# Transposing DMAs no longer serialized with plain DMAs, and two parameter loads in place of a touch read, in a statically scheduled SSM + SwiGLU kernel

## The chip, the cores and the metric

The kernel runs on one core of one Trainium2 chip. The metric is the device time of one execution in microseconds (us). The kernel before scattered by at most 0.33% within one set of rounds (179.78 to 180.37 us in the widest). A profile shows one execution, so where a kernel scatters it need not show the median one. Engines in the profile: PE is TensorE's matmuls, PEld its weight loads, DVE is VectorE, ACT is ScalarE, POOL is GpSimd, SP is SyncE, which here only issues DMAs. "SPq" and "ACTq" are DMA issues on the queue of that engine.

## The reference, cut to what matters

```python
# x: 2048 x 512; P = 512 complex states; F = 1376; everything bfloat16
x  = A_x
xn = _layernorm(x)
# A: diagonal state space model
Lam_bar = exp(exp(log_dt) * (Lambda_re + 1j*Lambda_im))
Bu   = xn @ (((Lam_bar - 1) / Lam)[:, None] * (B_re + 1j*B_im)).T
h    = scan over rows t:  h = Lam_bar * h + Bu[t]
a    = 2 * real(hseq @ (C_re + 1j*C_im).T) + xn * Dskip
# B: gated feed-forward
b    = (silu(xn @ w_gate) * (xn @ w_up)) @ w_down
out  = x + a + b
```

## The kernel before

The 2048 rows are 16 tiles of 128 rows, worked on in four chunks of four tiles. Each chunk needs: its load; the layer norm's statistics on VectorE and the norm itself (on ScalarE for chunks 2 and 3); a transpose of the normalized rows by DMA; the gate, up and B projections on TensorE; evacuations of PSUM by ScalarE (it copies TensorE's results out of tile `pb`, so that the next matmuls may write there); the rotation and scan on VectorE; and one accumulation on TensorE of the down projection ("dA") and of the state times the C weights ("dB"). The C weights (tile `W`) are computed once, on ScalarE and VectorE, from the transposed C (tile `hss`, lent for it) and the parameters.

Nothing is ordered by hand. The program is a graph of tasks; a list scheduler with a model of durations puts the tasks of ACT, DVE and POOL in an order, and PE and SP keep the order in which the program names them. Only then are the waits put in. So the instruction order on ScalarE and VectorE is an output of a model of when DMAs land. The parts that matter:

```python
_DMA_BW = 330.0        # bytes per ns in the model
_DMA_LAT = 2000.0      # ns
_CHAIN = ("pe", "sp")  # these keep program order
...
        # in _schedule, for the best candidate t of engine e that could start at st:
        if t.dma:
            issue_done = st + t.est
            xs = max(st + min(t.est, 300.0), dma_free[e])
            dma_free[e] = xs + t.nbytes / (_DMA_BW if e == "sp" else 0.5 * _DMA_BW)
            t.fin = dma_free[e] + _DMA_LAT
            free[e] = issue_done
...
        dma_tasks = []
        xp_state = [None]

        def dma(name, dst, src, writes, nbytes, ..., xpose=False, ...):
            after = tuple(after)
            if xpose:
                after = after + tuple(dma_tasks)          # a transpose waits for every DMA before it
                fn = ... dma_start_transpose ...
                est, nb = 2000.0, int(nbytes * 1.2)
            else:
                if xp_state[0] is not None:
                    after = after + (xp_state[0],)        # a plain DMA waits for the last transpose
                fn = ... dma_start ...
                est, nb = 330.0 + nbytes / 900.0, nbytes
...
        x_load(0)
        x_load(1)
        act_q = [dma("ld_touch", tch[0:16], wg_v[0:128:8, :, 0:2], [("tch",)], 16 * 16, eng="act")]
        act_q.append(wg_load("a0", 0, 2, eng="act", order=(act_q[-1],)))     # 448 KB of gate weights
        x_load(2)
        act_q.append(wg_load("a1", 2, 3, eng="act", order=(act_q[-1],)))     # 224 KB
        wg_load("a2", 3, 4)
        x_load(3)
        pload("ld_ldt", 2, A_log_dt)           # 1 KB each
        pload("ld_lim", 1, A_Lambda_im)
        pload("ld_lre", 0, A_Lambda_re)
        # then: up weights, rest of the gate weights, x tiles 4-7 ("x4"), B_re and B_im (transposes),
        # chunk 1's rows (transpose), C_re and C_im (transposes), x tiles 8-11 ("x8"), down weights, ...
...
        streams = _schedule(g.tasks, engs)      # fixes the order on ACT, DVE, POOL
        _plan(g.tasks, streams, new_sem, eng_sems)   # puts the semaphore waits in
```

The touch is a small read of `w_gate` (16 partitions, 8 elements each); nothing uses its result.

Of the kernel before, what the change touches and what calls it, by code (L numbers as in the profile page):

```python
# [12 lines left out]
B16 = mybir.dt.bfloat16  # L13
# [236 lines left out]
def bass_parallel_sum__ssm_conv_s5__swiglu_ffn__prompt_kernel(  # L250
# [23 lines left out]
    KT = D // 128  # L274
# [6 lines left out]
    g = _Graph()  # L281
    es = ExitStack()
    with es:
        block = es.enter_context(nc.Block(no_gpsimd_drain=True))

        def sb(name, shape, dt):
            return es.enter_context(nc.sbuf_tensor(name, shape, dt))
# [41 lines left out]
        st0 = sb("st0", [128, 4, 2, 6], F32)  # L329
        sd0 = sb("sd0", [128, 4], F32)  # L330
        epst = sb("epst", [128, 1], F32)
        tch = sb("tch", [16, KT, 2], B16)
        praw = sb("praw", [128, 3, PT], B16)
        prow = sb("prow", [12, 128], B16)
        ecst = sb("ecst", [128, PT], F32)
# [1 line left out]
        NSM = 64  # L337
        sm = sb("sm", [128, NSM, PT], F32)
# [46 lines left out]
        wg_v = B_w_gate.rearrange("(k p) f -> p k f", p=128)  # L385
        wu_v = B_w_up.rearrange("(k p) f -> p k f", p=128)

        dma_tasks = []
        xp_state = [None]

        def dma(name, dst, src, writes, nbytes, reads=(), after=(), out_=False, eng="sp", xpose=False, prio=0.0, order=(), **kw):
            after = tuple(after)
            if xpose:
                after = after + tuple(dma_tasks)
                fn = lambda e, dst=dst, src=src: e.dma_start_transpose(out=dst, in_=src)
                est, nb = 2000.0, int(nbytes * 1.2)
            else:
                if xp_state[0] is not None:
                    after = after + (xp_state[0],)
                fn = lambda e, dst=dst, src=src: e.dma_start(dst, src, **kw)  # L400
                est, nb = 330.0 + nbytes / 900.0, nbytes
            t = g.add(eng, fn, reads=reads, writes=writes, name=name, dma=True, after=after, out=out_, est=est, nbytes=nb, prio=prio, order=order)
            dma_tasks.append(t)
            if xpose:
                xp_state[0] = t
            return t

        TILEB = 128 * D * 2
# [4 lines left out]
        def pload(name, slot, src, **kw):  # L413
            return dma(name, prow[4 * slot:4 * slot + 4, :], src.rearrange("(a p) -> a p", p=128), [("prow", slot)], 1024, **kw)

        def x_load(a, **kw):
            return dma("ld_x%d" % a, x_sb[:, a:a + 1, :], x_v[:, a:a + 1, :], [("x", a)], TILEB, **kw)

        def wg_load(nm, k0, k1, **kw):
            return dma("ld_wg" + nm, wg[:, k0:k1, 0:FG], wg_v[:, k0:k1, 0:FG], [("wg", nm)], (k1 - k0) * 128 * FG * 2, **kw)  # L420

        x_load(0)
        x_load(1)
        act_q = [dma("ld_touch", tch[0:16], wg_v[0:128:8, :, 0:2], [("tch",)], 16 * 16, eng="act")]
        act_q.append(wg_load("a0", 0, 2, eng="act", order=(act_q[-1],)))
        x_load(2)
        act_q.append(wg_load("a1", 2, 3, eng="act", order=(act_q[-1],)))
        wg_load("a2", 3, 4)
        x_load(3)
        pload("ld_ldt", 2, A_log_dt)  # L430
        pload("ld_lim", 1, A_Lambda_im)
        pload("ld_lre", 0, A_Lambda_re)
        dma("ld_wu0", wu[:, :, 0:FH0], wu_v[:, :, 0:FH0], [("wu", 0)], 512 * FH0 * 2)
        dma("ld_wg1", wg[:, :, FG:Fh], wg_v[:, :, FG:Fh], [("wg", 1)], 512 * (Fh - FG) * 2)
# [7 lines left out]
        def loads_stage_b2():  # L442
# [13 lines left out]
              reads=[("ones",)], writes=[("ident",)], name="ident", est=300)  # L456
        g.add("pool", lambda e: e.iota(iot[:], pattern=[[1, TP]], base=0, channel_multiplier=0, allow_small_or_imprecise_dtypes=True),
              writes=[("iot",)], name="iota", est=1000)
# [1 line left out]
        g.add("pool", lambda e: e.memset(car[:, 0], 0.0), writes=[("car", 0, 0), ("car", 0, 1)], name="car0", est=100)  # L460
        g.add("pool", lambda e: e.memset(ecst[:], math.e), writes=[("ecst",)], name="ecst", est=100)
        def act_table(func, order):
            g.add("act", lambda e: e.activation(out=sm[:, NSM - 1, 0:1], in_=epst[:], func=func, bias=epst[:, 0:1]), reads=[("epst",)], writes=[("sm", "_warm")],
                  name="act_warm", est=1500, order=order)

        act_table(AF.Sqrt, (act_q[-1],))

        def pe_warm(n, w=512, bk=None):
# [295 lines left out]
        def ffn_gate_quarters(pairs):  # L764
# [27 lines left out]
            for a_, b_ in zip(seq, seq[1:]):  # L792
                hold[b_].od.add(hold[a_])
            act_table(AF.Silu, (hold["ev21"],))
            hold["evac"] = g.tasks[-1]
            ffn_mm(0, NQ, "g", xt_pair[0])
# [275 lines left out]
```

## Time and profile before

| | before |
|---|---|
| time, median of 3 | 179.94 us (179.92 to 180.0) |
| profiled span | 178.1 us |
| PE busy | 174.4 us (98%) |
| DVE busy | 162.3 us (91%) |
| waits of PE | 0.8 us, at the start only |
| x4 landed / x8 landed | 13.76 us / 40.26 us |
| last C weight ready / first dB matmul | 73.08 us / 75.06 us |

The busy shares, from the first part of the page:

```profile
PE 174.4 (98%) x929; PEld 84.1 (47%) x937; DVE 162.3 (91%) x281; ACT 88.8 (50%) x114; POOL 10.3 (6%) x21
```

All of PE's waits, from the view of waits. The columns are: what waited, on what, us in total, times, longest us.

```profile
PE pb L474 <- PEq L1057: 0.8, 1, 0.8
```

Two places of the chain that ended last, the first PE piece and the very end. The columns are start, length in us, and what it was. Between them the chain is PE throughout:

```profile
7.01 0.28 PE pb L568 x2
...
170.59 5.18 PE pb L953 x39
175.79 0.29 DVE x_sb L958
```

So TensorE is the bound: at the pace of this chain (64 projection matmuls in 13.81 us, 216 ns each, at a granted clock of 1.0) there is nothing to gain from 7.01 us to 175.8 us without taking matmuls away.

SP's timeline shows what serializing costs in DMA time. The columns are start, length of the issue, queue and line, operation and tiles:

```profile
5.81 0.55 SPq L400 DMA_DIRECT2D x_sb<-in_A_x_dram  x1
14.00 2.06 SPq L395 DMA_TRANSPOSE BT<-in_A_B_re_dram  x1
18.54 2.00 SPq L395 DMA_TRANSPOSE BT<-in_A_B_im_dram  x1
22.90 1.78 SPq L395 DMA_TRANSPOSE xnT<-xn_sb  x1
28.54 1.70 SPq L395 DMA_TRANSPOSE hss<-in_A_C_re_dram  x1
32.63 1.97 SPq L395 DMA_TRANSPOSE hss<-in_A_C_im_dram  x1
36.79 0.37 SPq L400 DMA_DIRECT2D x_sb<-in_A_x_dram  x1
```

Each transpose is issued only when all earlier loads have landed, so x8 is issued at 36.79 us. The statistics of those tiles stand late on VectorE, so it waits only 0.76 us for them (in brackets: idle before, and what ended it):

```profile
40.28 2.47 DVE L479 BATCH_NORM_STATS2 st<-x_sb 128x6 f32<-128x512 bf16 x4 [0.76 <-DMA x_sb<-in_A_x_dram]
```

The PSUM evacuations (L839, L841, L844) and the first silu of chunk 1 (L754) come first, then chunk 2's four norms (L503):

```profile
41.53 1.02 ACT L841 ACTIVATE uf<-pb 32x1024 bf16<-32x1024 f32 x1
42.64 1.22 ACT L844 ACTIVATE uf<-pb 64x512 bf16<-64x512 f32 x2
43.88 1.02 ACT L754 ACTIVATE sg<-pb 128x1024 bf16<-128x1024 f32 x1
45.95 2.93 ACT L503 ACTIVATE xn_sb<-x_sb,nmr,rstd 128x512 bf16<-128x512 bf16 x4 [1.04 <-DVE nmr L500]
```

### The profile page before, as it was taken

Reading aid. Unit: us, or ns where it says so; the run is one execution under the profiler, and the core shown is the slowest. Engines: PE = TensorE matmul, PEld = TensorE weight load, DVE = VectorE, ACT = ScalarE, POOL = GpSimd, SP = SyncE. Lnnn points to the kernel's source line nnn. Section 1 sums busy time; section 2 is a strip of 40 time slices with the busy share of each in tenths; the row PEclk is TensorE's granted clock in tenths of the full one; section 3 lists DMA queues with packets and bytes.
Section 4 is the critical chain, followed back from the end, with each engine's and each line's share of the span. In section 5 each row is a group of like instructions: output and inputs, shape, how many; then the busy total and the mean of one; then the engine's idle time right before and its main releaser. Section 6 shows DMA issues by size and latency. Waiting matters only on the chain.

```text
span 178.1 us, 2421 instructions
## 1 busy us (share of the span) xinstructions
PE 174.4 (98%) x929; PEld 84.1 (47%) x937; DVE 162.3 (91%) x281; ACT 88.8 (50%) x114; POOL 10.3 (6%) x21
## 2 busy tenths in 40 slices
PE   8999999999999999999999999999999999999994
PEld 2794444444444444444444444444444444444743
DVE  2958984889799999989999999999999999999983
ACT  4469999999799948016565651000965620000000
POOL 3023300002200000050000000000000000000000
PEclk9999999999999999999999999999999999999999
DMA  5995593669260000001330000001100000000123
GB/s 168 377 328 117 119 118 74 136 179 346 88 121 0 0 0 0 0 31 61 86 64 0 0 0 4 0 0 59 59 0 4 0 0 0 0 0 4 59 77 100
DMA packets 22978, 12.37 MB, mean 69 GB/s; under 512 B 15192, under 2 KB 22968, under 8 KB 22968
## 3 DMA queue, kind: packets, MB, share of 16 engines
q1 hardware_dynamic: 22472, 11.54, 24.9%
q10 hardware_dynamic: 496, 0.69, 1.1%
q8 instruction: 7, 0.11, 0.3%
q14 instruction: 3, 0.02, 0.0%
HBM read 6.46 MB, written 2.10 MB: 48 GB/s over the span
## 4 chain that ended last, share of the span: by engine, by line
PE 95%; DVE 2%; DMA 1%; issue 0%; ACT 0%
PE pb L742 36%; PE pb L940 21%; PE pb L857 16%; PE pb L953 15%; PE pb L783 3%; PE pb L820 2%; DMA x_sb<-in_A_x_dram 1%; PE pb L830 1%; PE pb L568 1%; DVE xn_sb L514 1%; DVE st L527 0%; DVE st L509 0%; ACT sd L521 0%; DVE mv L519 0%; DVE rstd L530 0%
## 5 line engine op out<-in xcount | busy, mean ns | idle before, releaser
L897 DVE TENSOR_TENSOR_SCAN rot<-sm,car,rot 128x512 bf16<-128x512 f32 x32 | 38.9, 1266 | 0.1
L940 PE MATMUL pb<-wd,hT 128*128 128x512 bf16 (+3 forms) x194 | 38.1, 355 | 0.2
L742 PE MATMUL pb<-xnT,wu 128*128 128x512 bf16 x160 | 37.3, 379 | 0.0
L742 PE MATMUL pb<-xnT,wg 128*128 128x512 bf16 x132 | 31.3, 379 | 0.0
L953 PE MATMUL pb<-W,hss 128*128 128x512 bf16 (+2 forms) x140 | 28.1, 355 | 0.2
L857 PE MATMUL pb<-xnT,BT 128*128 128x512 bf16 x128 | 28.1, 379 | 0.0
L940 PEld LDWEIGHTS pb<-wd,hT 128*128 128x128 bf16 (+1 forms) x198 | 18.5, 98 | 19.9
L742 PEld LDWEIGHTS pb<-xnT,wu 128*128 128x128 bf16 x160 | 15.6, 98 | 18.9 <-issue 0.2
L754 ACT ACTIVATE sg<-pb 128x1024 bf16<-128x1024 f32 x20 | 20.2, 1025 | 8.3 <-PE pb L742 7.2
L810 ACT ACTIVATE uf<-pb 128x1024 bf16<-128x1024 f32 x20 | 20.6, 1029 | 6.8 <-PE pb L742 6.7
L953 PEld LDWEIGHTS pb<-W,hss 128*128 128x128 bf16 x144 | 13.4, 98 | 14.3
L742 PEld LDWEIGHTS pb<-xnT,wg 128*128 128x128 bf16 x132 | 12.7, 98 | 15.7 <-issue 0.8
L857 PEld LDWEIGHTS pb<-xnT,BT 128*128 128x128 bf16 x128 | 12.5, 98 | 15.1
L864 ACT ACTIVATE u_sb<-pb 128x1024 bf16<-128x1024 f32 x16 | 16.4, 1027 | 4.6 <-PE pb L857 4.2
L812 DVE TENSOR_TENSOR hT<-sg,uf 128x1024 bf16<-128x1024 bf16 x20 | 13.5, 682 | 0.8 <-ACT uf L810 0.6
L888 DVE TENSOR_TENSOR rot<-u_sb,cosT 128x2048 bf16<-128x2048 bf16 x8 | 9.7, 1218 | 2.9 <-ACT cosT L703 2.9
L958 DVE TENSOR_TENSOR x_sb<-pb,x_sb 128x512 bf16<-128x512 f32 (+2 forms) x18 | 10.8, 622 | 1.2 <-PE pb L953 1.2
L839 ACT ACTIVATE sg<-pb 96x1024 bf16<-96x1024 f32 x2 | 2.0, 1021 | 17.3 <-PE pb L820 17.3
L503 ACT ACTIVATE xn_sb<-x_sb,nmr,rstd 128x512 bf16<-128x512 bf16 x8 | 5.9, 803 | 9.6 <-DVE nmr L500 9.6
L888 DVE TENSOR_TENSOR rot<-rot,cosT 128x2048 bf16<-128x2048 bf16 x8 | 9.7, 1215 | 0.1
L888 DVE TENSOR_TENSOR rot<-rot,sin 128x2048 bf16<-128x2048 bf16 x8 | 9.7, 1216 | 0.0
L888 DVE TENSOR_TENSOR rot<-u_sb,sin 128x2048 bf16<-128x2048 bf16 x8 | 9.7, 1216 | 0.0
(78 smaller groups left out, 144.3 us busy)
## 6 DMA issues: line engine op xcount, KB each, us to landing
out_dram<-x_sb SPq DMA_DIRECT2D x15, 128.0 KB, 1.7
x_sb<-in_A_x_dram SPq DMA_DIRECT2D x3, 512.0 KB, 7.6
wd<-in_B_w_down_dram SPq DMA_DIRECT2D x1, 1280.0 KB, 7.1
wu<-in_B_w_up_dram SPq DMA_DIRECT2D x1, 768.0 KB, 5.0
wu<-in_B_w_up_dram SPq DMA_DIRECT2D x1, 608.0 KB, 7.1
x_sb<-in_A_x_dram SPq DMA_DIRECT2D x4, 128.0 KB, 3.3
wg<-in_B_w_gate_dram SPq DMA_DIRECT2D x1, 480.0 KB, 6.0
wg<-in_B_w_gate_dram ACTq DMA_DIRECT2D x1, 448.0 KB, 3.8
```

Of the source, the lines that this page charges most:

```text
L503: g.add("act", lambda e, a=a: e.activation(out=xn_sb[:, a % NXN, :], in_=x_sb[:, a, :], func=AF.Identity, scale=rstd[:, a:a + 1], bias=nmr ...
L742: inst = e.matmul(pbank[0:fs, bk, :].rearrange("p (j t) -> p j t", j=4), lhsT=w[:, kt, i * 128:i * 128 + fs], rhs=xnT[:, c % 2, :, kt, :], ...
L754: g.add("act", lambda e: e.activation(out=sg[rows, sl, 0:n, :].rearrange("p a t -> p (a t)"), in_=pair_f32(rows, bk, 512 * n), func=AF.Sil ...
L810: g.add("act", lambda e: e.activation(out=uf[rows, ul, 0:n, :].rearrange("p a t -> p (a t)"), in_=pair_f32(rows, bk, 512 * n), func=AF.Ide ...
L812: g.add("dve", lambda e: e.tensor_tensor(out=hT[rows, hb, i0:i0 + n, :], in0=sg[rows, sl, 0:n, :], in1=uf[rows, ul, 0:n, :], op=ALU.mult), ...
L857: inst = e.matmul(pbank[:, bk, :].rearrange("p (j t) -> p j t", j=4), lhsT=BT[:, ri, kt, pt * 128:(pt + 1) * 128], rhs=xnT[:, c % 2, :, kt ...
L864: g.add("act", lambda e: e.activation(out=u_sb[:, us].rearrange("p r t -> p (r t)"), in_=pair_f32(slice(0, 128), b0), func=AF.Identity), r ...
L888: tt = lambda out, a, b, op, r, w, nm: g.add("dve", lambda e: e.tensor_tensor(out=out, in0=a, in1=b, op=op), reads=r, writes=w, name="%s_% ...
L897: g.add("dve", lambda e, A0=A0, A1=A1, k=k, ri=ri, pt=pt: e.tensor_tensor_scan(out=A1[:, k, ri, :], data0=rr[:, pt:pt + 1].to_broadcast([1 ...
L940: inst = e.matmul(pbank[:, bk, 0:nc_], lhsT=hT[0:fs, hb, i, lt * 128:(lt + 1) * 128], rhs=wd[0:fs, i, c0:c0 + nc_], start=(i == 0), stop=F ...
L953: inst = e.matmul(pbank[:, bk, 0:nc_], lhsT=hss[:, hb, pt, ri, lt * 128:(lt + 1) * 128], rhs=W12[:, ri, pt, c0:c0 + nc_], start=False, sto ...
L958: g.add("dve", lambda e, bk=bk, a=a, c0=c0, nc_=nc_: e.tensor_tensor(out=x_sb[:, a, c0:c0 + nc_], in0=pbank[:, bk, 0:nc_], in1=x_sb[:, a, ...
```

## The change

The intent: to have transposes and plain loads in flight together, so that SP does not wait around each transpose and everything behind it comes sooner. And the touch gives way to two loads that are needed anyway. They come to ScalarE's queue ahead of the gate weights and leave SP's queue.

```diff
-        dma_tasks = []
-        xp_state = [None]
 
         def dma(name, dst, src, ...):
             after = tuple(after)
             if xpose:
-                after = after + tuple(dma_tasks)
                 fn = ... dma_start_transpose ...
                 est, nb = 2000.0, int(nbytes * 1.2)
             else:
-                if xp_state[0] is not None:
-                    after = after + (xp_state[0],)
                 fn = ... dma_start ...
@@
-        act_q = [dma("ld_touch", tch[0:16], wg_v[0:128:8, :, 0:2], [("tch",)], 16 * 16, eng="act")]
+        act_q = [pload("ld_ldt", 2, A_log_dt, eng="act")]
+        act_q.append(pload("ld_lim", 1, A_Lambda_im, eng="act", order=(act_q[-1],)))
         act_q.append(wg_load("a0", 0, 2, eng="act", order=(act_q[-1],)))
@@
-        pload("ld_ldt", 2, A_log_dt)
-        pload("ld_lim", 1, A_Lambda_im)
         pload("ld_lre", 0, A_Lambda_re)
@@ (the warm activation loses its bias operand; the tile tch goes)
-            ... activation(out=..., in_=epst[:], func=func, bias=epst[:, 0:1])
+            ... activation(out=..., in_=epst[:], func=func)
```

All transposes stay on SP's queue; the change mixes them with plain DMAs, not with transposes of another engine. What the diff does not show: with those dependencies gone from the graph, the scheduler also computes a new order for ScalarE and VectorE.

More of the change, by code (lines that the diff above doesn't have):

```diff
@@ L331, in bass_parallel_sum__ssm_conv_s5__swiglu_ffn__prompt_kernel @@
         epst = sb("epst", [128, 1], F32)
-        tch = sb("tch", [16, KT, 2], B16)
         praw = sb("praw", [128, 3, PT], B16)
@@ L402, in dma @@
             t = g.add(eng, fn, reads=reads, writes=writes, name=name, dma=True, after=after, out=out_, est=est, nbytes=nb, prio=prio, order=order)
-            dma_tasks.append(t)
-            if xpose:
-                xp_state[0] = t
             return t
@@ L462, in act_table @@
         def act_table(func, order):
-            g.add("act", lambda e: e.activation(out=sm[:, NSM - 1, 0:1], in_=epst[:], func=func, bias=epst[:, 0:1]), reads=[("epst",)], writes=[("sm", "_warm")],
+            g.add("act", lambda e: e.activation(out=sm[:, NSM - 1, 0:1], in_=epst[:], func=func), reads=[("epst",)], writes=[("sm", "_warm")],
                   name="act_warm", est=1500, order=order)
```

## The prediction

> **What bounds the kernel now.** TensorE. The page has it busy 174.4 us of 178.1 us (98%). In the chain of waits PE holds 95%, and from 7.01 us to 175.8 us the chain is PE without a break, except for 0.02–0.05 us of issue. That busy time is also at pace: the chain gives 13.81 us for 64 projection matmuls (216 ns each), 17.37 us for 80 gate/up matmuls (217 ns), granted clock 1.0 throughout. Before 7.01 us the chain is the load of tile 0 (0.79 to 3.04 us) and the first layer norms on DVE and ACT. After 175.8 us it is the last addition and store. Only these two ends can become shorter; the change touches only the first.
>
> VectorE is the second limit: 162.3 us (91%), and the timeline shows it nearly gapless from 49 us to 171 us. The last elementwise state (L888, hss) ends at 168.35 us, and its first reader on PE starts at 168.65 us: about 0.3 us of slack. So DVE time lost early on and not recovered would show at the end; DVE time gained buys slack only.
>
> **What the change removes.** The SP queue's waits around transposes: in SP's view of waits 11.2 us on the input loads, 3.8 on the transposed activations, 2.5 + 2.4 + 2.3 + 2.2 us on the parameter transposes. B_re's transpose (issued at 14.00) should be issued at about 5.5–6.5 us, B_im's right after; the chunk-1 activation transpose at about 20 us (now 22.90; its inputs are ready at 19.9), C_re and C_im from about 22 us (now 28.54 and 32.63), the x8 load at about 26 us (now 36.79). None of these has PE waiting now: PE's view of waits has only 0.8 us at the start. B's transposes are read from 24.75 us, after landing at about 22.8 us. DVE may lose its 0.76 us wait for the x8 tiles (40.28) and perhaps the 0.86 us for POOL behind it. [...]
>
> **What it adds and moves.** On ACT's queue one touch issue (0.41 us) becomes two small loads (on SP they took 0.25–0.37 us each): about +0.3 us before the gate loads, the table load (2.23 → about 2.5) and the warm activation, which would end at about 4.1 us. The first sd activation started at 4.01 us after its DVE input, so it slips about 0.1 us, and this lies on the chain: the first PE transposes, now 4.94, go to about 5.05. The gate weights land at about 5.0 us (issue plus 3.8) and are read at 6.01: 0.3 us later they are still in time. SP is freed of 0.7 us of issue, off the chain. In 7–13.5 us the DMA engines are 99% busy, so earlier transposes share with the last loads; those have slack. The static order of DVE and ACT instructions is recomputed from a model in which transposes land earlier; a bad order is the main risk.
>
> **Predicted: 180.0 us**, range 179.6 to 180.7; faster by over 2%: 0.005, within 2%: 0.98, slower by over 2%: 0.015.
>
> **What would show it.** Right: PE still gapless from about 7.1 us at 216 ns a matmul; transposes issued as above with PE's waits unchanged; SP's transpose waits gone; sd at about 4.1 us. Wrong: PE waits on gate weights near 6 us (the touch did matter), on a PSUM evacuation, or on hss before the last matmuls; or a start that became shorter.
>
> **What would make it wrong.** A reordering that puts DVE or ACT behind a late transfer; transposes slowing the plain loads much when mixed; a first transfer that lands late without the touch.

The sum is 179.94 us before plus about 0.1 us for the first `sd`, put down as 180.0 us.

## The result, and the profile after

| | before | after |
|---|---|---|
| median, same rounds | 179.93 us | 181.75 us (181.42 to 182.69, 6 runs) |
| ratio | | 1.0109, 95% interval 1.0082 to 1.0135 |
| profiled span | 178.1 us | 179.8 us |

By the 2% rule the verdict is "same", but the interval excludes 1: the change made the kernel 1.8 us slower. The result is correct, in this run and in every run below. The prediction's class was right, and its range (179.6 to 180.7) does not hold the time.

Line numbers after are about ten lower: L469 is the L479 of before, L493 is L503, L732 is L742, L831 is L841.

The shares of the chain by engine (where before had PE 95%):

```profile
PE 73%; DMA 7%; SPq 6%; DVE 6%; ACT 4%; POOL 2%; issue 1%; ACTq 0%; DVEq 0%
```

PE's waits, where before had only the 0.8 us at the start:

```profile
PE pb L464 <- PEq L1047: 0.8, 1, 0.8
PE pb L732 <- ACT uf L831: 0.6, 1, 0.6
PE pb L773 <- DMA wg<-in_B_w_gate_dram: 0.4, 1, 0.4
...
PE pb L732 <- ACT u_sb L854: 0.2, 1, 0.2
```

SP's timeline shows that the freed transposes are indeed issued sooner, and that the issues themselves became long:

```profile
5.80 1.47 SPq L394 DMA_DIRECT2D x_sb<-in_A_x_dram  x1
7.32 7.43 SPq L391 DMA_TRANSPOSE BT<-in_A_B_re_dram  x1
14.80 2.82 SPq L391 DMA_TRANSPOSE BT<-in_A_B_im_dram  x1
20.70 1.82 SPq L391 DMA_TRANSPOSE xnT<-xn_sb  x1
22.56 2.56 SPq L391 DMA_TRANSPOSE hss<-in_A_C_re_dram  x1
25.17 3.26 SPq L391 DMA_TRANSPOSE hss<-in_A_C_im_dram  x1
28.47 0.58 SPq L394 DMA_DIRECT2D x_sb<-in_A_x_dram  x1
```

x8 lands at 32.43 us, almost 8 us sooner than before. Yet VectorE now waits *longer* for it, because its new order reaches the statistics at 29.5 us:

```profile
32.46 2.47 DVE L469 BATCH_NORM_STATS2 st<-x_sb 128x6 f32<-128x512 bf16 x4 [2.94 <-DMA x_sb<-in_A_x_dram]
```

ScalarE's new order has the norms of those tiles ahead of, and between, the PSUM evacuations (L854, L829, L831). So it stands 3.59 us with nothing else that it may do:

```profile
34.08 1.02 ACT L854 ACTIVATE u_sb<-pb 128x1024 bf16<-128x1024 f32 x1
38.69 0.81 ACT L493 ACTIVATE xn_sb<-x_sb,nmr,rstd 128x512 bf16<-128x512 bf16 x1 [3.59 <-DVE nmr L490]
39.41 1.00 ACT L854 ACTIVATE u_sb<-pb 128x1024 bf16<-128x1024 f32 x1
...
45.28 1.02 ACT L831 ACTIVATE uf<-pb 32x1024 bf16<-32x1024 f32 x1
```

And TensorE needs the `pb` that L831 frees. On PE's timeline the matmuls end, wait 0.64 us and go on at 46.35 us. This is the third group of eight gate matmuls of chunk 1 ("third gate group" below). It ran at 44.83 us before. Before, then after:

```profile
44.83 1.89 PE L742 MATMUL pb<-xnT,wg 128*128 128x512 bf16 x8
...
43.82 1.89 PE L732 MATMUL pb<-xnT,wu 128*128 128x512 bf16 x8
46.35 1.90 PE L732 MATMUL pb<-xnT,wg 128*128 128x512 bf16 x8 [0.64 <-ACT uf L831]
```

The chain that ended last, as the profile follows it, says it in one piece. PE is not in it until 46 us. It runs from the x4 load over VectorE to SP's two C transposes, the x8 load, the statistics, the norm, the evacuations, and only then to PE:

```profile
5.80 9.21 DMA x_sb<-in_A_x_dram
15.03 2.47 DVE st L469 x4
...
25.17 3.26 SPq L391
28.43 0.04 issue
28.47 3.96 DMA x_sb<-in_A_x_dram
32.46 2.47 DVE st L469 x4
...
45.28 1.03 ACT uf L831
46.30 0.05 issue
46.35 13.99 PE pb L732 x64
```

From there to the end PE is gapless again. In every profile but two the last matmul ends 100.7 us after the first dB matmul (before: 75.06 to 175.76; after: 76.73 to 177.44), so the time of the first dB matmul is a good measure of what was lost before it. The two are front_only (101.1 us) and after_cfirst_norms (102.5 us).

### The profile page after: what moved, and what is told of

Its sections match the earlier page's. It is cut to its first block, busy times and chain, and to the rows that moved or that the text cites. A ratio compares the mean times of both kernels' runs of the same rounds, so it can differ in the third digit from the quotient of the medians.

```text
span 179.8 us, 2416 instructions
## 1 busy us (share of the span) xinstructions
PE 174.8 (97%) x937; PEld 83.8 (47%) x937; DVE 161.8 (90%) x281; ACT 87.9 (49%) x114; POOL 10.0 (6%) x21
## 4 chain that ended last, share of the span: by engine, by line
PE 73%; DMA 7%; SPq 6%; DVE 6%; ACT 4%; POOL 2%; issue 1%; ACTq 0%; DVEq 0%
PE pb L732 27%; PE pb L930 21%; PE pb L943 15%; PE pb L847 8%; DMA x_sb<-in_A_x_dram 7%; SPq L391 3%; DVE st L469 3%; SPq L394 3%; ACT xn_sb L493 2%; ACT u_sb L854 2%; POOL rstd L481 1%; PE pb L810 1%; DVE xn_sb L485 1%; DVE hT L802 1%; POOL ve L477 1%
## 5 line engine op out<-in xcount | busy, mean ns | idle before, releaser
L930 PE MATMUL pb<-wd,hT 128*128 128x512 bf16 (+3 forms) x198 | 38.8, 355 | 0.0
L732 PE MATMUL pb<-xnT,wu 128*128 128x512 bf16 x160 | 37.3, 379 | 0.0
L732 PE MATMUL pb<-xnT,wg 128*128 128x512 bf16 x132 | 31.3, 379 | 0.8 <-ACT uf L831 0.6
L943 PE MATMUL pb<-W,hss 128*128 128x512 bf16 (+2 forms) x144 | 28.3, 355 | 0.0
L732 PEld LDWEIGHTS pb<-xnT,wu 128*128 128x128 bf16 x160 | 15.7, 98 | 18.9 <-issue 0.2
L732 PEld LDWEIGHTS pb<-xnT,wg 128*128 128x128 bf16 x132 | 12.6, 98 | 16.8 <-ACT uf L831 1.1
L847 PEld LDWEIGHTS pb<-xnT,BT 128*128 128x128 bf16 x128 | 12.5, 98 | 15.1
L854 ACT ACTIVATE u_sb<-pb 128x1024 bf16<-128x1024 f32 x16 | 16.5, 1028 | 4.2 <-PE pb L847 3.9
L469 DVE BATCH_NORM_STATS2 st<-x_sb 128x6 f32<-128x512 bf16 x12 | 7.5, 680 | 5.0 <-DMA x_sb<-in_A_x_dram 5.0
L493 ACT ACTIVATE xn_sb<-x_sb,nmr,rstd 128x512 bf16<-128x512 bf16 x8 | 6.2, 805 | 9.3 <-DVE nmr L490 9.3
L829 ACT ACTIVATE sg<-pb 96x1024 bf16<-96x1024 f32 x2 | 2.0, 1016 | 17.1 <-PE pb L810 17.1
```

The lines of the kernel that those rows point to most:

```text
L469: return g.add("dve", lambda e, a=a: e.bn_stats(out=st[:, a, :], in_=x_sb[:, a, :]), reads=[("x", a)], writes=[("st", a)], name="bnst%d" % ...
L732: inst = e.matmul(pbank[0:fs, bk, :].rearrange("p (j t) -> p j t", j=4), lhsT=w[:, kt, i * 128:i * 128 + fs], rhs=xnT[:, c % 2, :, kt, :], ...
L847: inst = e.matmul(pbank[:, bk, :].rearrange("p (j t) -> p j t", j=4), lhsT=BT[:, ri, kt, pt * 128:(pt + 1) * 128], rhs=xnT[:, c % 2, :, kt ...
L854: g.add("act", lambda e: e.activation(out=u_sb[:, us].rearrange("p r t -> p (r t)"), in_=pair_f32(slice(0, 128), b0), func=AF.Identity), r ...
L930: inst = e.matmul(pbank[:, bk, 0:nc_], lhsT=hT[0:fs, hb, i, lt * 128:(lt + 1) * 128], rhs=wd[0:fs, i, c0:c0 + nc_], start=(i == 0), stop=F ...
L943: inst = e.matmul(pbank[:, bk, 0:nc_], lhsT=hss[:, hb, pt, ri, lt * 128:(lt + 1) * 128], rhs=W12[:, ri, pt, c0:c0 + nc_], start=False, sto ...
```

## The experiments

Three theories stood after the traces were read:

- **Order:** the scheduler's new order for ScalarE and VectorE, computed from too early landings, costs the time.
- **Mixing:** transposes and plain loads in flight together slow each other, and this costs the time whatever the order.
- **Front:** the two parameter loads ahead of the gate weights cost the time (gate weights late, x4 late).

Later ones are named where they come up. For the experiments the two uses of the serializing were pulled apart, so that it can be in the scheduler's model and in the emitted waits separately, and the order of ACT, DVE and POOL can be pinned to that of another kernel:

```diff
-                after = after + tuple(dma_tasks)
+                ser = set(dma_tasks)          # likewise for plain DMAs: ser = {xp_state[0]}
 ...
+            ser_of[t] = ser - t.deps
 ...
+        if MODEL: t.deps |= ser_of[t]         # for every DMA task, for the scheduler only
         streams = _schedule(g.tasks, engs)
+        t.deps -= ser_of[t]; if WAITS: t.deps |= ser_of[t]     # for the emitted waits
+        streams = {act, dve, pool tasks in the pinned order}   # where pinned
         _plan(g.tasks, streams, new_sem, eng_sems)
```

### First: one half of the change at a time

**unser_order_old.** Before, MODEL = True, WAITS = False: only the waits around transposes go; loads and instruction order stay.

> The kernel before, every instruction in its old order, only the waits that serialize the transposes taken out. Theory A: 179.8 to 180.1, no new wait of TensorE. Rival C: 181 or more.

Measured: 179.86 us, ratio 1.0001 (0.9989 to 1.0013). x8 landed at 31.73 us, PE has no wait but that at the start. Taking the waits out is worth nothing, as predicted, and costs nothing.

**unser_only.** Before, MODEL = False, WAITS = False: the unserialized half with the order that its scheduler computes; the touch and the old loads stay.

> The kernel before with only the serialization of transposes removed (in the scheduler's model and in the waits); touch and parameter loads as before. Theory A: no wait on gate weights; VectorE blocked 2 to 3 us near 29 us by a tile-8 load that the order expects too early, ScalarE's norms between PSUM evacuations, TensorE waiting about 0.5 to 1.2 us near 42 to 47 us: 180.5 to 181.1. Rival B: both losses are here, also a wait on gate weights near 7.7 us: 181.5 or more.

Measured: 179.93 us, 1.0005 (0.9992 to 1.0018), x8 at 31.66 us. The expected 180.5 to 181.1 us was missed: VectorE did wait 2.68 us for x8 and ScalarE 1.49 us for the norms, and PE lost nothing. So a wait of VectorE for x8 is not a loss by itself; what counts is what stands behind it. An order computed from the early landings does not have to cost anything (run by itself, the scheduler of this kernel has x8 at 29.4 us on its model's clock); this one has its norms a little further back among the evacuations, the last of them behind the first silu of chunk 1, and its last C weight ends 43.0 us after x8.

**unser_order_new.** After, MODEL = True, WAITS = False: all of the change's loads and waits, but the order of a serialized model.

> The whole change in what is transferred and waited for, but the static order of VectorE and ScalarE is computed with the serialized transposes in the model (the order of front_only). Theory A (the order is the cause of the middle loss): as front_only, 180.3 to 180.6, TensorE without a wait near 44 us. Rival C (the unserialized transfers themselves cost, whatever the order): as the changed kernel, 181.4 or more.

Measured: 179.92 us, 1.0003 (0.9991 to 1.0015), x8 at 32.02 us, no PE wait on ScalarE or a DMA. These are the change's own DMAs on the chip, and they cost nothing. Mixing falls: B_re's issue is no shorter here (8.25 us) than after the change (7.43), and no one has to wait for it.

**front_only.** Before with the change's loads, still serialized (its scheduler computes the order).

```diff
-        act_q = [dma("ld_touch", ...)]
+        act_q = [pload("ld_ldt", 2, A_log_dt, eng="act")]
+        act_q.append(pload("ld_lim", 1, A_Lambda_im, eng="act", order=(act_q[-1],)))
@@
-        pload("ld_ldt", 2, A_log_dt)
-        pload("ld_lim", 1, A_Lambda_im)
```

> The kernel before with only the queue front of the change: the touch out, two parameter loads first on ScalarE's queue and off SP's; transposes stay serialized. Theory A (two separate causes: late gate weights at the start, and a changed static order in the middle): only the early loss is here, about +0.5 us: 180.3 to 180.6, TensorE waits 0.3 to 0.6 us on the gate weights near 7.7 us and nowhere near 44 us. Rival B (the front is harmless, the early transposes share the DMA engines with the gate loads and delay them): 179.9 and no wait on gate weights.

Measured: 181.28 us (180.23 to 182.71), 1.0082 (1.0052 to 1.0112). That is more than the 180.3 to 180.6 us expected. So the front is no bystander: where transposes are still serialized, the front and the order that the scheduler computes for it cost 1.4 us. x4 landed at 14.73 us instead of 13.76, and since everything behind it waits in line, x8 landed at 41.58. VectorE's longest wait for such a load went from 0.76 to 2.9 us. PE waited 0.7 us on gate weights and 0.5 on an evacuation. Its VectorE order is not that of before (58 of 281 instructions stand at another place), so the loads alone are not isolated here. unser_order_new has exactly this order and this front, and costs nothing once the waits are gone. So the price depends on the slack behind x8. No run has the full new front with the order of before.

### Second: what of the front, and is the order alone enough?

**after_again.** The changed kernel once more, as a control in the rounds of the next three runs.

> The changed kernel again, unaltered, as the control on the chip and in the rounds of the other runs of this call. Both theories: 181.4 to 182.7 as in its first rounds. If it is under 180.2 here, the loss depends on the chip or the day and not on the program.

Measured: 181.7 us (181.07 to 182.65), 1.0102. The same, with one difference in the profiled run: the 0.4 us wait for gate weights near 7.7 us was absent, and the waits between 40 and 47 us were longer (0.17 + 0.56 + 0.64 us, against 0.15 + 0.64). The early wait, where it comes, is swallowed by the later one; the two do not add up.

**after_touch.** The changed kernel, with the touch put back ahead of the two loads, and its order pinned.

```diff
-        act_q = [pload("ld_ldt", 2, A_log_dt, eng="act")]
+        act_q = [dma("ld_touch", ...)]
+        act_q.append(pload("ld_ldt", 2, A_log_dt, eng="act", order=(act_q[-1],)))
```

> The changed kernel with every instruction in its place, and the touch read put back ahead of the two parameter loads on ScalarE's queue; the gate loads are issued about 0.4 us later still. Theory T (the touch made the first packets of the gate loads fast): the gate loads land as early as in the changed kernel or up to 1 us earlier although issued later, little or no TensorE wait on them near 7.7 us, 179.9 to 181.0. Rival Q (what counts is how late the gate loads are issued, the touch does nothing): they land about 0.4 us later than in the changed kernel, TensorE waits about 1 us on them, 181.8 or more.

Measured: 181.25 us (181.11 to 181.87), 1.0080. The touch does not bring the gate weights back: they landed at 6.75 and 7.5 us, against 6.01 and 7.72 after the change, and far from the 5.0 and 5.94 of before. So what the touch itself does is not what was lost. The time lies between the ranges of both theories.

**front_notouch.** Before without the touch; nothing put in its place.

> The kernel before with only the touch read left out; order, waits and SP's queue as before; the first gate load is issued 0.44 us earlier. Theory T: its packets are slow at first, it lands no earlier than before (about 5.0 us) or later, and the loads behind it no earlier; 179.9 to 181. Rival Q: it lands about 0.4 us earlier, near 4.6 us, and the time is 179.8 to 179.9.

Measured: 180.48 us (180.34 to 181.77), 1.0042 (1.0020 to 1.0065). Here the gates were issued and landed earlier (4.6 and 5.59 us instead of 5.0 and 5.94), but tile 1 of x landed at 4.95 us instead of 4.11. PE waited 1.2 us for the first norms. So the gate loads came forward by 0.4 us and this load of x went back by 0.84 us; that the one pushed the other is not shown by one profile.

**after_norms_late.** The changed kernel with its order pinned, except that ScalarE's four norms go back to where they were before, behind the first silu of chunk 1.

```diff
 ACT: ... tm2 uev_b1_0
-     xn8 uev_b1_1 xn9 uev_b1_2 xn10 uev_b1_3 xn11 silul0 uevx0 uevl0_0 uevl0_1 silu1_0
+     uev_b1_1 uev_b1_2 uev_b1_3 silul0 uevx0 uevl0_0 uevl0_1 silu1_0 xn8 xn9 xn10 xn11
```

> The changed kernel with one edit to ScalarE's static order: the four norms of tiles 8 to 11 go back behind the first gate evacuation of chunk 1, where they stood before; VectorE's order, the loads and the waits stay. Theory O (ScalarE stands in front of PSUM evacuations, waiting for norms whose tiles land later than the scheduler's model says): the waits of TensorE near 42 to 46 us go, 180.3 to 180.7, only the wait on gate weights stays. Rival D (VectorE, blocked about 3 us by the same tiles, is what costs): 181.3 or more, with TensorE waiting on VectorE later.

Measured: 181.86 us (181.49 to 184.0), 1.0130 (1.0092 to 1.0167): no gain at all. The third gate group runs at 44.81 us again, as before, but later PE waits on something else, of which the changed kernel's waits had no trace:

```profile
PE pb L943 <- DVE W L707: 1.5, 1, 1.5
```

The C weights now come last. The chain named after the change was one of two of equal length.

### Third: two chains from one load

Both chains begin at x8's landing. In the changed order ScalarE's norms and evacuations let PE run the third gate group, from which it is 30.4 us of gapless PE to the first dB (46.35 to 76.73). And VectorE, 97% busy from there on (42.94 of the 44.30 us from 32.4 to 76.7), ends the last C weight. The distances are the same wherever this order runs:

| kernel with after's order | x8 landed | third gate group | distance | last C weight | distance |
|---|---|---|---|---|---|
| after | 32.43 | 46.35 | 13.92 | 76.68 | 44.25 |
| after_again | 32.55 | 46.47 | 13.92 | 76.80 | 44.25 |
| after_touch | 32.20 | 46.08 | 13.88 | 76.40 | 44.20 |
| after_norms_late (ScalarE's chain cut) | 32.46 | 44.81 | | 76.64 | 44.18 |
| oldfront_afterorder | 31.46 | 45.33 | 13.87 | 75.65 | 44.19 |

13.9 + 30.4 is 44.3: the two ends meet. Looked at closely, VectorE's end came last: the first dB starts 0.05 to 0.06 us after the last C weight wherever this table shows both chains, and where the C weights are early the stretch of PE takes 30.2 us (before, 44.83 to 75.06) and not 30.4. So the C weights held PE for some 0.15 us, too little for the profile's view of waits, and the chain that it followed was the other. Before, PE was ready for the first dB at 75.06 us and the last C weight at 73.08. The last C weight before and after:

```profile
72.33 0.75 DVE L717 SCALAR_TENSOR_TENSOR W<-hss,sm,scrC 128x512 bf16<-128x512 bf16 x1
...
75.93 0.74 DVE L707 SCALAR_TENSOR_TENSOR W<-hss,sm,scrC 128x512 bf16<-128x512 bf16 x1
```

**oldfront_afterorder.** The unserialized half with the old loads, and the changed kernel's order pinned: the order alone.

> The kernel before with the serialization of transposes removed and its old queue front (touch, parameter loads on SP), but VectorE and ScalarE in exactly the static order of the changed kernel. Theory O (the order is the cause; in three profiles of that order TensorE's third gate group of chunk 1 starts 13.9 us after the tile-8 load lands): the load lands near 31.7 us, TensorE resumes near 45.6 us where it would be at 44.9, 180.4 to 180.8. Rival F (the new queue front is the cause): no wait, 179.8 to 180.0.

Measured: 180.57 us (180.5 to 181.06), 1.0045 (1.0031 to 1.0059). x8 at 31.46, first dB at 75.71. The order costs 0.7 us with the old front.

**newfront_unserorder.** The changed kernel with the order of unser_only pinned.

> The changed kernel with all its loads and waits, but VectorE and ScalarE in the order that the scheduler gave unser_only (there the four norms stand one place later on ScalarE, the last of them behind a gate evacuation). Theory O: the tile-8 load lands near 32.5 us, 0.8 us later than in unser_only, and ScalarE's slack of about 1 us takes it up: 179.9 to 180.3, at most a short wait on gate weights near 7.7 us. Rival F: 181 or more, as every kernel with this front and its own order but unser_order_new.

Measured: 180.23 us (180.02 to 180.65), 1.0021 (1.0008 to 1.0033). x8 at 32.24, first dB at 75.26.

Together with the runs above this makes a table of unserialized kernels:

| median us (x8 landed) | order of a serialized model | unser_only's order | after's order |
|---|---|---|---|
| old front | 179.86 (31.73) | 179.93 (31.66) | 180.57 (31.46) |
| new front | 179.92 (32.02) | 180.23 (32.24) | 181.75 (32.43) |

In the first column the two orders are not the same: the old front has the order of before, the new front that of front_only. The second and third columns each have one order throughout. Neither half costs much by itself; together they cost 1.8 us. From oldfront_afterorder to after, x8 lands 0.97 us later and the first dB runs 1.02 us later: with this order, a late x8 goes into the time one for one.

**after_both_late.** As after_norms_late, and VectorE's statistics of tiles 8 to 11 moved behind its first scan, as before.

```diff
 DVE: ... tzc1
-     bnst8 ... bnag11  pin1_0_0 pin2_0_0 nmr8 ... scan0_0_0
+     pin1_0_0 pin2_0_0 ... scan0_0_0  bnst8 ... bnag11
```

> after_norms_late with one more edit: VectorE's statistics of tiles 8 to 11 go back behind the first scan, where they stood before; nothing else. Theory O: both engines then do other work until the tiles land; TensorE waits neither near 44 us nor for the C weights near 77 us, 179.9 to 180.3. Rival: another part of the new order costs as well, over 180.8.

Measured: 181.06 us (181.05 to 181.26), 1.0069. The rival was right here. VectorE no longer waits for x8 (which landed at 33.68 us), yet the last C weight ends at 76.20 us, only 0.48 us sooner, and PE still waits 1.1 us on it. Putting the waiting elsewhere is not enough. The next runs ask whether other work that after's order has put ahead of the C weights has to go as well.

**after_cfirst.** The changed order, but the C weights go ahead of what had overtaken them on VectorE (statistics of tiles 12 to 15 and a residual addition; some 3.6 us), as before.

```diff
 DVE:
-     ... bnst12 ... bnst15, rs2_0 in front of the C weights ... w1_3 w2_3 bnag12
+     ... w1_3 w2_3 rs2_0 bnst12 bnst13 bnst14 bnst15 bnag12
```

> The changed kernel with one edit to VectorE's static order: the eight C-weight instructions come ahead of the statistics of tiles 12 to 15 and the second residual step of chunk 0, as they did before; ScalarE's order stays. Theory two-chains (in the new order two chains of equal length start at the landing of tile 8: over ScalarE's norms to the third gate group, +13.9 us, and from there 30.4 us of TensorE to the first product with the C weights; and over VectorE to the last C weight, +44.2 us): mending VectorE's alone gains little, the last C weight is ready near 73 us, TensorE still waits near 42 to 46 us, 181.2 to 182.5. Rival (VectorE's order is the whole cause): 179.8 to 180.4.

Measured: 181.15 us (180.93 to 181.93), 1.0075. The C weights end at 75.0 us instead of 76.68, and the first dB still runs at 76.24: this leaves ScalarE's chain (third gate group at 45.99, 13.91 us after x8).

**after_cfirst_norms.** Both: norms back, C weights first.

> The edits of after_norms_late and after_cfirst together; the statistics of tiles 8 to 11 stay early on VectorE. Theory two-chains: both chains are out of the way, the last C weight is ready near 73 us, TensorE waits on neither, 179.8 to 180.3, although neither edit alone gains. Rival: over 180.8.

Measured: 180.42 us (180.19 to 181.63), 1.0035 (1.0014 to 1.0056). Now the third gate group runs at 44.81 and the first dB at 75.05 us, as before. Each mend alone gained 0.6 us or nothing, both together 1.3. The expected 179.8 to 180.3 us was narrowly missed. The profile is of the slowest of the six executions (181.63 us; the others took 180.19 to 180.57), so its late waits of PE show what that one lost and not what the median lost:

```profile
PE pb L732 <- DVE x_sb L948: 0.7, 1, 0.7
...
PE pb L943 <- DVE hss L878: 0.4, 1, 0.4
```

The last state (`hss`) is ready at 170.36 us there, and at 168.35 before with PE needing it at 168.65: in that execution VectorE's 0.3 us of slack was spent. Where the other executions lost their 0.3 to 0.7 us is not shown.

**after_est35.** The changed kernel with one number of the model corrected: a transpose's issue occupies SP's queue for 3500 ns in place of 2000.

```diff
-                est, nb = 2000.0, int(nbytes * 1.2)
+                est, nb = 3500.0, int(nbytes * 1.2)
```

> The changed kernel with one number changed: the scheduler's model takes 3500 ns in place of 2000 ns for the issue of a transpose (the profile of the changed kernel has 7.4, 2.8, 1.8, 2.6 and 3.3 us), so that it puts the tile-8 load at 32.8 us (28.3 before; it landed at 32.43), and the order follows from that. Theory O: the waits of VectorE and ScalarE for these tiles go or become short and TensorE loses little, 179.9 to 180.4. Rival: as the changed kernel, 181.4 or more.

Measured: 179.86 us (179.82 to 179.99), 1.0000 (0.9987 to 1.0012), with the change's loads, waits and transposes all in place. x8 lands at 32.27 us, as after, but the order is another one. ScalarE does two of the four norms ahead of L829 and the others behind L834; the last C weight ends at 74.89, the first dB runs at 75.07. VectorE does not wait for x8 at all (2.94 us after the change), and ScalarE waits 0.58 us for the first norm (3.59). PE's waits are those of before:

```profile
PE pb L464 <- PEq L1047: 0.8, 1, 0.8
```

Running the kernel's own scheduler shows what changed in its model. These are its landing times, against those of the traces. The model's clock starts with the kernel's first instruction, which in the trace is at 0.8 us:

| | model before | trace before | model after | trace after | model est35 | trace est35 |
|---|---|---|---|---|---|---|
| x4 | 13.1 | 13.76 | 12.5 | 15.01 | 12.5 | 14.93 |
| x8 | 38.4 | 40.26 | 28.3 | 32.43 | 32.8 | 32.27 |

Before, serialization kept the model honest: x8 stood behind the same chain of waits in the model and in the trace, and landed at 38.4 and 40.26 us. After, the model lets SP issue the two C transposes for 2.0 us each from 20.4 us on. In the trace they took 2.56 and 3.26 us from 22.56 us on, and x8 came 4.1 us after the model's time, of which 0.8 is the difference of the clocks, some 1.3 the later start of these two issues and some 1.8 their length. One corrected number was tried, once. unser_only shows that a harmless order can come from an uncorrected model too, so this run shows that the order was the loss, and not that a better model always finds a better order. The 3500 ns are about the mean of the changed kernel's five issues (7.43, 2.82, 1.82, 2.56 and 3.26 us: 3.6).

### Fourth: the last open points

**ser_afterorder.** Before with all of its waits and the old front, but the changed kernel's order pinned. If the order lives on an early x8, then an x8 at 41 us must hurt badly.

> The kernel before with all its waits (transposes serialized, old queue front) and only the static order of VectorE and ScalarE taken from the changed kernel. Theory two-chains: the tile-8 load lands near 40.3 us, TensorE resumes 13.9 us later at 54.2 us, 9.3 us after its time, 188.5 to 190. Rival (the order matters little): under 182.

Measured: 190.09 us (188.83 to 191.47, 4 runs), 1.0566 (1.0521 to 1.0610), just above the 188.5 to 190 us expected. x8 landed at 41.27 us in the profiled run (191.47 us), and the last C weight ended 44.20 us later, as in the table above. ScalarE stands 12.80 us in front of the first norm, and PE waits for an evacuation as in the changed kernel, only longer:

```profile
49.26 1.92 PE L830 MATMUL pb<-xnT,wu 128*64 128x512 bf16 x8 [8.73 <-ACT u_sb L864]
51.11 3.59 PE L742 MATMUL pb<-xnT,wg 128*128 128x512 bf16 x8
```

The second line also has a side effect: these 8 matmuls took 3.59 us; in the other traces 8 of the same kind take 1.89 to 1.90. The mean granted clock was 0.67 from 45 to 60 us, and 1.00 from 20 to 40 and from 60 to 80. So much slower, PE itself became the later chain here: the third gate group ran at 56.46 us, 15.2 us after x8 and not 13.9. The lower clock is seen around the end of the 8.73 us wait (at 49.26 us); that the wait caused it was not tested. In the changed kernel, whose waits after the start are 0.64 us and less, the clock stayed at 1.0.

**unser_params_last.** Unserialized, before's order pinned, touch kept, and the two parameter loads on ScalarE's queue *behind* the gate weights: do gate weights come in time, with SP's queue still freed of those loads?

```diff
         act_q.append(wg_load("a1", 2, 3, eng="act", order=(act_q[-1],)))
+        act_q.append(pload("ld_ldt", 2, A_log_dt, eng="act", order=(act_q[-1],)))
+        act_q.append(pload("ld_lim", 1, A_Lambda_im, eng="act", order=(act_q[-1],)))
```

> The kernel before, in its own static order, transposes not serialized, touch kept; the two parameter loads go to ScalarE's queue behind the gate loads and not ahead of them, so SP's queue is freed as in the change. Theory Q (the time at which the gate loads are issued sets their landing, and they pull the other loads with them): the gate loads land at about 5.0 and 6.0 us as before, 179.8 to 180.0. Rival S (SP's large loads, issued 0.6 us earlier, push the gate loads back): the second gate load lands at 6.5 us or later.

Measured: 180.40 us (180.39 to 180.42), 1.0025 (1.0013 to 1.0038): the expectation missed. The larger gate load was in time (4.93 us), but ScalarE was not. Its timeline:

```profile
2.23 0.58 ACTq L402 DMA_DIRECT2D prow<-in_A_log_dt_dram  x1
2.84 0.28 ACTq L402 DMA_DIRECT2D prow<-in_A_Lambda_im_dram  x1
3.15 1.28 ACT L466 ACT_TABLE_LOAD   x1 [3.15 <-issue]
...
4.65 0.28 ACT L524 ACTIVATE sd<-mv,epst 128x1 f32<-128x1 f32 x1
```

Two issues of 1 KB push the table load from 2.23 to 3.15 us and the first `sd`, which is on the chain, from 4.01 to 4.65. PE's first transpose goes from 4.94 to 5.56 us. The run gives 0.5 us for a reason that the changed kernel does not have (its `sd` is at 4.06).

Why the gate weights and x4 land 1.0 to 1.8 us later after the change, for an issue of the gate weights only 0.44 us later, **stays open**. The touch is not the reason (after_touch). The smaller gate load landed at 7.13 us in unser_params_last, where SP's following loads are issued earlier, which would fit a theory that those push it back. But on the same chip ser_afterorder, with the old front, had 6.90 us against 5.94 in the first profile of before. Between 3 and 4 us the DMA engines moved 326 GB/s before and 186 after, and 218 in unser_order_new, which ran at 179.92: a slow start goes with the new front, and its cause was not found.

## Why the prediction was right or wrong

- *TensorE bounds the kernel, and none of the removed waits "has PE waiting now".* Right. unser_order_old and unser_only took the waits out and ran at 179.86 and 179.93 us.
- *Transposes are issued earlier.* Right in kind. B_re was said for 5.5 to 6.5 us and was issued at 7.32; chunk 1's rows 20 (20.70); C_re 22 (22.56); x8 26 (28.47). The sum missed that the issues get longer: 7.43 us for B_re instead of 2.06, and 2.56 + 3.26 for C instead of 1.70 + 1.97 (2.15 us more, and the x8 load stands behind them on SP). Why they get longer is not shown here.
- *"sd at about 4.1 us", first PE transposes "to about 5.05".* Right: 4.06 and 5.06.
- *Gate weights "0.3 us later they are still in time".* Mis-sized: they landed at 6.01 and 7.72 us (before 5.0 and 5.94), and PE waited 0.4 us in one profile, none in the repeat. This did not decide the time.
- *"DVE may lose its 0.76 us wait for the x8 tiles", and PE is "still gapless".* **This is the step that failed:** the new order was counted as free. The wait became 2.94 us, PE waited 0.15 us at 42.09 and 0.64 us at 46.35, the last C weight came at 76.68 in place of 73.08, and the first dB moved by 1.67 us (75.06 to 76.73). The prediction named "a reordering that puts DVE or ACT behind a late transfer" as what would make it wrong, and then put 0 us for it into its sum. It measured +0.7 us with the old front (oldfront_afterorder) and, with x8 1.0 us later by the new front, another 1.1. The scheduler is in the kernel's source, so its new order and its landing times could have been written down beside the trace's before predicting.

The best kernels tie with before (after_est35 at 179.86 us, with the whole change in place). None beats it, which fits a PE that is packed from 7.01 us to 175.8 us.

## What to carry to other kernels

When instruction order comes from a model, a change to DMA dependencies is a change to the order: the scheduler may spend at once the slack that it believes it has won (it did here, and not in unser_only), so compare the model's landing times with the trace's before and after, and pin the order to tell transfers from order. When a mend of the chain that ended last gains nothing, look for a second chain of the same length from the same start (here ScalarE's evacuations and VectorE's C weights), and mend both. Here one corrected number in the model removed both. Where the bound engine is already packed, earlier loads have little to give (x8 8.5 us sooner in unser_order_old, at 179.86 us as before), and the new order that comes with them can take (1.8 us here).
